# Five products of the first expert's first layer in another order, in a fused state-space scan and expert layer

## The chip, the cores and the metric

The kernel runs on one core of one Trainium2 chip. The metric is the device time of one execution, in microseconds (us); less is better. In the views below PE is TensorE's matmul, PEld its weight load, DVE is VectorE, ACT is ScalarE, POOL is GpSimd, and SP is SyncE, which only issues DMAs here.

## What is computed

First comes a chunked state-space scan (its result y has 3072 rows of 256 numbers), then an expert layer: every token goes to one of eight experts by a hash of its number, and through that expert's two matrices.

```python
# scan, 4 x 8 heads, 768 steps in chunks of 32
L = np.exp(cum[:, :, :, None] - cum[:, :, None, :]) * causal
y_intra = np.einsum('bhij,bhjd->bhid', CB * L, xc)
y_inter = np.einsum('bhin,bhnd->bhid', Cc, state) * decay_to_i[..., None]
...
# experts: x is (3072, 256), w1[e] is 256 x 1024, w2[e] is 1024 x 256
expert_idx = token_ids * np.int64(2654435761) % np.int64(E)
for e in range(E):
    xe = x[expert_idx == e]
    out[expert_idx == e] = np.maximum(xe @ w1[e], 0.0) @ w2[e]
```

All matmuls of the expert layer are in float32.

## The kernel before

Up to about 74 us the core computes the scan, works out which token goes where, and writes y to DRAM. POOL's indirect DMAs (`gather`, line 628) bring the rows of y back in the order of the experts, 128 rows to a tile; PE transposes them (`turn_x`, line 636) and ACT copies them into `xT`, which holds the tokens as columns. The experts are sorted by their number of tokens into places p = 0 to 7. Place p has two halves of `HALF[p]` columns: 202 for place 0, 200 for place 1.

Each matrix product of an expert is a product of 2 x 2 blocks: two halves of the inputs, two halves of the outputs, two halves of the tokens. It is computed with seven block products in place of eight. They work on sums of weight blocks (`sums_w`, line 782: `s[0]` to `s[3]`) and on differences of token blocks (`sums_x`, line 882), which build on each other:

```python
# sums_x: a, b of t[i] = a - b; q(k, j) is input half k of token half j
a_, b_ = ((q(0, 1), q(0, 0)), (q(1, 1), t[:, 0]), (q(0, 1), q(1, 1)), (q(1, 0), t[:, 1]))[i]
```

In `up` (line 903), the first layer, product 1 and 2 use tokens as they are, 5 uses `s[0]` and `t[0]`, 6 uses `s[1]` and `t[1]`, 7 uses `s[2]` and `t[2]`, 4 uses a weight block and `t[3]`, 3 uses `s[3]` and tokens. Each product is made in two halves (`q0` = 0 and 2), of two matmuls each; a float32 matmul shows as two records in the profile. I call them 5a and 5b and so on. The a halves use PSUM banks 0 and 1, the b halves 2 and 3: products 1, 2, 5 and 3 stand in bank 0 (2), products 6, 7 and 4 in bank 1 (3), where 7 adds onto 6 and 4 onto 7. Each result is read before the next product adds onto it: after 6 (`u2`, line 932) and 7 (`u3`, line 935) DVE adds product 1's part, then product 5's bank and `u3` give a block of the hidden layer (line 944), 4 gives another (line 941), 3 the third (line 939). ACT applies the relu to the first two (lines 945, 942).

For the first four places, products 1 and 2 are made early, while DVE still makes weight sums (line 1049; bank `i % 6`). The last four of these halves belong to place 3: its a half stands in bank 0, its b half in bank 1, and ACT reads them (product 2: line 927).

Then `step(p)` (line 1059) walks over the places. It puts the first layer of place p beside the second layer of place p - 1 (`down`, line 964) on PE, in an order written out in lists: `UP_E` (line 1056) has the five products that are left for the first four places. Step 0 has no second layer beside it: its rounds are a half a, a transposed tile of place 1's tokens, a half b (lines 1081 and 1091). Between them `step` puts the differences for the next place (`sums_x(1, i)`, line 1107) on DVE, and weight sums for later on POOL. In step 1, `sums_h` (lines 891 to 898) makes the differences of the hidden layer of place 0 on DVE. The order on each engine is the order in which this code is written; waits between engines are set by the tiles and banks that instructions share.

Of the kernel before, what the change touches and what calls it, by code (L numbers as in the profile page):

```python
# [20 lines left out]
NEAR = 4  # L21
# [4 lines left out]
def kernel(  # L26
# [20 lines left out]
    E, _, F = moe_w1.shape  # L47
# [564 lines left out]
    def load_w1(p, i, eng=sp_e):  # L612
        if p not in w1s:
            w1s[p] = (w4[0] if p % 4 == 3 else wpool).tile([P, DP, F], F32, name="w1")
        src = moe_w1[bass.ds(regs[p], 1), :, i * FH:(i + 1) * FH].rearrange("e (k p) f -> p (e k) f", p=P)
        eng.dma_start(out=w1s[p][:, :, i * FH:(i + 1) * FH], in_=src)

    def load_w2(p, eng=sp_e):
        w2s[p] = wx[0].tile([P, FP, DM], F32, name="w2", bufs=2)
        eng.dma_start(out=w2s[p], in_=moe_w2[bass.ds(regs[p], 1)].rearrange("e (k p) d -> p (e k) d", p=P))  # L620
# [144 lines left out]
    def sums_w(p, layer, i, eng):  # L765

        if layer == 1:
            w = w1s[p]
            q = lambda i, k: w[:, k, i * FH:(i + 1) * FH]
            if p not in s1:  # L770
                s1[p] = (spool if p % 3 else s1pool).tile([P, 4, FH], F32, name="s1")
            s = s1[p]
        else:
            w = w2s[p]
            q = lambda i, k: w[:, k * Q4:(k + 1) * Q4, i * P:(i + 1) * P]
            if p not in s2:
                s2[p] = spool.tile([P, 4, Q4, P], F32, name="s2")
            s = s2[p]
        i = (2, 1, 3, 0)[i]
        a_, b_, o = ((q(1, 0), q(1, 1), OP.add), (s[:, 2], q(1, 1), OP.add), (q(1, 0), q(0, 0), OP.subtract),  # L780
                     (q(0, 1), s[:, 1], OP.subtract))[i]
        eng.tensor_tensor(out=s[:, i], in0=a_, in1=b_, op=o)  # L782
        if eng is pool_e and i in (0, 3):
            eng.tensor_copy(out=space, in_=s[:, i, 0, 0:1] if layer == 2 else s[:, i, 0:1])
# [90 lines left out]
    def sums_x(p, i):  # L875
        n = HALF[p]
        q = lambda k, j: xT[:, k, slots(p, j)]
        if i == 0:
            t1[p] = mwork.tile([P, 4, N0], F32, name="t1")
        t = t1[p][:, :, 0:n]  # L880
        a_, b_ = ((q(0, 1), q(0, 0)), (q(1, 1), t[:, 0]), (q(0, 1), q(1, 1)), (q(1, 0), t[:, 1]))[i]
        dve.tensor_tensor(out=t[:, i], in0=a_, in1=b_, op=OP.subtract)  # L882

    def sums_h(p, i):
        n = HALF[p]
        if i == 0:
            t2[p] = hpool.tile([P, 4, Q4, N0], F32, name="t2", bufs=1)
        t = t2[p][:, :, :, 0:n]
        q = lambda k, j: hx[p][:, {(0, 1): 0, (1, 0): 1, (1, 1): 2}[k, j], :, 0:n]
        if i == 0:  # L890
            dve.scalar_tensor_tensor(out=t[:, 0], in0=q(0, 1), scalar=0.0, in1=h11[p][:, :, 0:n],
                                     op0=OP.max, op1=OP.subtract)
        elif i == 1:
            dve.tensor_tensor(out=t[:, 1], in0=q(1, 1), in1=t[:, 0], op=OP.subtract)
        elif i == 2:
            dve.scalar_tensor_tensor(out=t[:, 2], in0=q(0, 1), scalar=0.0, in1=q(1, 1), op0=OP.max, op1=OP.subtract)  # L896
        else:
            dve.tensor_tensor(out=t[:, 3], in0=q(1, 0), in1=t[:, 1], op=OP.subtract)
# [90 lines left out]
    def put(k, bank=OB, at=0, eng=None):  # L989
        for i in range(DP):  # L990
            pe.transpose(out=ps[:, bank, at + i * P:at + (i + 1) * P], in_=xT[:, i, k * P:(k + 1) * P], identity=ident)  # L991
        o_sb = mwork.tile([P, DM], F32, name="o_sb", bufs=10)
        if eng is dve:
            dve.tensor_copy(out=o_sb, in_=ps[:, bank, at:at + DM])
        else:
            act.activation(o_sb, ps[:, bank, at:at + DM], AF.Copy)  # L996
        return o_sb, idx_out[:, k:k + 1]

    def scatter(o_sb, idx):
        st = pool_e.indirect_dma_start(  # L1000
            out=out[:], out_offset=bass.IndirectOffsetOnAxis(ap=idx, axis=0),
            in_=o_sb, in_offset=None, bounds_check=NT - 1, oob_is_err=False)
        tc.declare_no_dep(st.ins, group="out_rows", reason="distinct rows")
        tc.add_to_no_dep_group("out_rows", st.ins)
# [6 lines left out]
    def ask(ks):  # L1011
        for k in ks:
            if k not in asked:
                gather(k)
                asked.add(k)

    def turn(k):
        if k not in turned:
            turn_x(k, XB)
            turned.add(k)  # L1020
# [33 lines left out]

    UP = [1, 6, 2, 7, 5, 4, 3]
    UP_E = [6, 7, 5, 4, 3]
    DOWN = [1, 2, 6, 5, 7, 4, 3]

    def step(p):

        ups = [] if p == E else UP_E if p < NEAR else UP
        downs = DOWN if p > 0 else []
        turns = [k for k in need(p + 1) if k not in turned]
        puts = [k for k in outs if done_at[k] == p - 2]
        gets = [k for w in ((2,), (3, 4))[p] for k in need(w) if k not in asked] if p < 2 else need(p + 3)
        sums = [(p, 2, i) for i in range(4)] if p < E else []
        sums += [(p + 2, 1, i) for i in range(4)] if 0 < p < E - 2 else []
        xs_ = [(p + 1, i) for i in range(4)] if p + 1 < E else []
        R = 5 if p == 0 else 7
        off = 0 if p == 0 else (R - len(ups)) // 2  # L1070
        sent = []
        for r in range(R):
            if p > 0 and (r == 0 or p >= NEAR and r < 4):
                sums_h(p - 1, r)
            if sent:
                scatter(*sent.pop(0))
            if gets and p == 0:
                ask(gets)
                gets = []
            if 0 <= r - off < len(ups):  # L1080
                up(p, 0, ups[r - off])
            if turns:
                turn(turns.pop(0))
            if puts:
                sent.append(put(puts.pop(0)))
            if sums and not (p == 1 and r < 4):
                sums_w(*sums.pop(0), pool_e)
            if gets and r >= 1:
                ask([gets.pop(0)])
            if 0 <= r - off < len(ups):  # L1090
                up(p, 2, ups[r - off])
            if 0 < p < NEAR and 0 < r < 4:
                sums_h(p - 1, r)
            if sums and r == 3 and p != 1:
                sums_w(*sums.pop(0), pool_e)
            if p >= NEAR and r >= 3 and not turns and xs_:
                sums_x(*xs_.pop(0))
            if p == 1 and r == 4:
                pool_e.tensor_copy(out=space, in_=t2[0][:, 3, 0, 0:1])
            if p == E - 1 and r == R - 1:  # L1100
                sums_h(p, 0)
            if downs:
                down(p - 1, downs[r])
                if downs[r] == 4 and p + 1 < E:
                    load_w2(p + 1)
            if p < NEAR and r >= (2 if p == 0 else 3) and not turns and xs_:
                sums_x(*xs_.pop(0))
        while xs_ or turns:
            if turns:
                turn(turns.pop(0))  # L1110
            else:
                sums_x(*xs_.pop(0))
        for o in sent:
            scatter(*o)
        for v in sums:
            sums_w(*v, pool_e)
        if p + 4 < E:
            load_w1(p + 4, 0)
            load_w1(p + 4, 1)
        for k in gets:  # L1120
            ask([k])

    for p in range(E):
        step(p)
# [136 lines left out]
```

## Time and profile before

| what | us |
|---|---|
| median of 3 runs | 235.72 |
| the runs | 231.1, 235.72, 237.67 |
| the profiled execution | 231.41 |
| its span, first to last instruction | 229.7 |
| PE busy | 213.5 (93%) |
| DVE busy | 180.7 (79%) |
| POOL busy | 172.4 (75%) |
| ACT busy | 89.4 (39%) |

The mean granted clock of TensorE is 0.992 of full speed in this execution. Times in the rows below count from the start of the span. A row of the timeline gives a start, a length, the engine, the line, the operation with the tiles that it writes and reads, how many instructions in a row it stands for, and in brackets the idle time ahead of it with what ended that. Lengths of PE's rows overlap, since matmuls are pipelined: the pace is read from one start to the next.

### The profile page before, as it was taken

The numbers are of one execution on the slowest core, as the hardware profiler recorded it, in microseconds if no ns is written. First come the engines' busy times: TensorE is split into PE (matmuls) and PEld (weight loads), VectorE is DVE, ScalarE is ACT, GpSimd is POOL, SyncE is SP. The second block draws the span as 40 slices with busy tenths as digits, with TensorE's granted clock in tenths as the row PEclk, the third lists the DMA queues.
The fourth block names the chain that finished last, engine by engine and source line by source line (L and its number), as shares of the span: only waits on it lengthen the run. The fifth ranks groups of instructions, "written<-read, shape, count | busy, mean of one in ns | idle before, by whom it ended". The sixth has DMA issues, their size and how long they took to land.

```text
span 229.7 us, 5853 instructions
## 1 busy us (share of the span) xinstructions
PE 213.5 (93%) x2266; PEld 200.5 (87%) x2266; DVE 180.7 (79%) x314; ACT 89.4 (39%) x190; POOL 172.4 (75%) x220
## 2 busy tenths in 40 slices
PE   6889989998786899999999999999999999999990
PEld 2778878877685799999999999999999999999980
DVE  7868899798547688899997998697489979956630
ACT  4774965954443551312123214234323411413210
POOL 7977367866717198489988998999799999996342
PEclk9999999999999999999999999999999999999996
DMA  6999799999888885029019119307005112401011
GB/s 136 162 200 127 181 191 177 174 185 302 273 218 259 253 267 199 24 75 332 30 62 334 64 47 339 118 7 244 26 24 204 33 45 79 175 23 47 24 70 43
DMA packets 49877, 33.16 MB, mean 144 GB/s; under 512 B 26632, under 2 KB 44184, under 8 KB 49850
## 3 DMA queue, kind: packets, MB, share of 16 engines
q1 hardware_dynamic: 46786, 25.76, 45.6%
q0 software_dynamic: 2400, 6.43, 8.5%
q10 hardware_dynamic: 664, 0.61, 1.1%
q8 instruction: 18, 0.29, 0.5%
q14 instruction: 9, 0.07, 0.1%
HBM read 26.49 MB, written 6.42 MB: 143 GB/s over the span
## 4 chain that ended last, share of the span: by engine, by line
PE 73%; DMA 8%; DVE 7%; ACT 6%; issue 2%; SPq 1%; POOL 1%; ACTq 0%; DVEq 0%; POOLq 0%
PE ps L964 31%; PE ps L917 28%; PE ps L315 4%; DMA w<-in_moe_w_dram 3%; DMA xg<-y_tokens,idx_in 3%; PE ps L991 2%; PE ps L374 2%; PE ps L636 2%; DMA y_tokens<-y_sb 2%; DVE m L321 1%; ACT z L358 1%; PE ps L387 1%; PE ps L269 1%; DVE rows L259 1%; ACT ct L289 1%
## 5 line engine op out<-in xcount | busy, mean ns | idle before, releaser
L628 POOL DMA_INDIRECT xg<-y_tokens,idx_in x25 | 30.2, 1206 | 17.1 <-issue 10.1
L917 PE MATMUL ps<-t,s 128*128 128x202 f32 (+7 forms) x192 | 37.1, 328 | 0.6 <-DVE t L882 0.6
L782 POOL TENSOR_TENSOR s<-w 128x512 f32<-128x512 f32 x26 | 33.2, 1277 | 5.7 <-DMA w<-in_moe_w_dram 5.5
L1000 POOL DMA_INDIRECT out_dram<-o_sb,idx_out x25 | 26.4, 1056 | 12.5 <-ACT o_sb L996 6.7
L964 PE MATMUL ps<-t,s 128*128 128x202 f32 (+7 forms) x192 | 35.5, 326 | 0.0
L917 PEld LDWEIGHTS ps<-t,s 128*128 128x128 f32 x192 | 31.5, 190 | 1.3 <-ACT h L927 0.9
L964 PEld LDWEIGHTS ps<-t,s 128*128 128x128 f32 x192 | 31.8, 189 | 0.3 <-issue 0.3
L917 PE MATMUL ps<-xT,w 128*128 128x200 f32 (+7 forms) x128 | 24.9, 329 | 3.0 <-DMA w<-in_moe_w_dram 2.3
L917 PEld LDWEIGHTS ps<-xT,w 128*128 128x128 f32 x128 | 20.7, 190 | 3.8 <-DVE s L782 2.5
L945 ACT ACTIVATE hx<-hx 128x404 f32<-128x404 f32 (+7 forms) x16 | 8.3, 525 | 31.8 <-DVE hx L944 31.3
L321 DVE COPY_PREDICATED m<-cmask,ps 128x1024 f32<-128x1024 int32 x12 | 15.5, 1320 | 3.6 <-PE ps L315 3.6
L782 POOL TENSOR_TENSOR s<-w,s 128x512 f32<-128x512 f32 x13 | 17.6, 1351 | 0.5
L782 POOL TENSOR_TENSOR s<-s,w 128x512 f32<-128x512 f32 x13 | 17.3, 1327 | 0.5
L882 DVE TENSOR_TENSOR t<-xT 128x202 f32<-128x202 f32 (+7 forms) x16 | 16.4, 1024 | 0.8 <-ACT xT L642 0.8
L923 ACT ACTIVATE p<-ps 128x404 f32<-128x404 f32 (+7 forms) x16 | 7.9, 492 | 20.0 <-PE ps L917 19.7
L374 PEld LDWEIGHTS ps<-x_t,m 128*64 128x64 f32 x384 | 12.1, 138 | 3.0 <-issue 1.3
L374 PE MATMUL ps<-x_t,m 128*64 128x64 f32 x384 | 13.4, 224 | 1.1 <-ACT y_sb L401 0.6
L315 PE MATMUL ps<-ce,bt 32*64 32x128 f32 x384 | 12.9, 274 | 1.1 <-ACT ce L289 0.7
L882 DVE TENSOR_TENSOR t<-xT,t 128x202 f32<-128x202 f32 (+7 forms) x16 | 13.7, 854 | 0.0
L896 DVE SCALAR_TENSOR_TENSOR t<-hx 128x808 f32<-128x808 f32 (+7 forms) x8 | 13.3, 1660 | 0.0
L315 PEld LDWEIGHTS ps<-ce,bt 32*64 32x64 f32 x384 | 10.4, 132 | 2.5 <-ACT ce L289 0.9
L358 ACT ACTIVATE z<-z,half 128x256 f32<-128x256 f32 x22 | 10.0, 504 | 6.6 <-DVE z L352 6.6
(201 smaller groups left out, 472.5 us busy)
## 6 DMA issues: line engine op xcount, KB each, us to landing
w<-in_moe_w_dram SPq DMA_DIRECT2D x16, 512.0 KB, 7.1
w<-in_moe_w_dram SPq DMA_DIRECT2D x8, 1024.0 KB, 8.0
x_t<-in_x_dram SPq DMA_DIRECT2D x12, 256.0 KB, 6.2
y_tokens<-y_sb SPq DMA_DIRECT2D x10, 256.0 KB, 4.3
raw<-in_B_dram SPq DMA_DIRECT2D x12, 128.0 KB, 3.5
raw<-in_C_dram SPq DMA_DIRECT2D x12, 128.0 KB, 3.5
y_tokens<-y_sb ACTq DMA_DIRECT2D x2, 256.0 KB
xg<-y_tokens,idx_in POOLq DMA_INDIRECT x25, 3.5
```

Source lines behind the costliest of these rows:

```text
L315: pe.matmul(out=ps[u * T:(u + 1) * T, GB + g, b * P:(b + 1) * P].rearrange("q (e i) -> q e i", e=2), lhsT=bts[ck][r, b, c], rhs=ces[ck][r, ...
L321: dve.copy_predicated(out=m_sb[k % 2][:, g0:g1].rearrange("q g b i -> q g (b i)"), mask=cmask.bitcast(I32).rearrange("q j i -> q (j i)").u ...
L358: act.activation(z4s[un][:, :, j], zs[un].rearrange("q b e d -> q b (e d)"), AF.Copy, scale=half4[:, j:j + 1])
L374: pe.matmul(out=o, lhsT=m_sb[k % 2][:, g, b, e * T:(e + 1) * T], rhs=xs[k][:, b, 2 * g + e], start=first(g // 2 * 2 + b % 2, c), stop=True ...
L628: pool_e.indirect_dma_start(out=xg[k], out_offset=None, in_=y_dram[0:n, :], in_offset=bass.IndirectOffsetOnAxis(ap=idx_in[:, k:k + 1], axi ...
L782: eng.tensor_tensor(out=s[:, i], in0=a_, in1=b_, op=o)
L882: dve.tensor_tensor(out=t[:, i], in0=a_, in1=b_, op=OP.subtract)
L896: dve.scalar_tensor_tensor(out=t[:, 2], in0=q(0, 1), scalar=0.0, in1=q(1, 1), op0=OP.max, op1=OP.subtract)
L917: pe.matmul(out=ps[:, bank, i * n:(i + 1) * n], lhsT=lhs[:, (q0 + i) * P:(q0 + i + 1) * P], rhs=rhs, start=(first and i == 0), stop=True, ...
L945: act.activation(hq(2), hq(2), AF.Relu)
L964: pe.matmul(out=ps[:, bank, 0:n], lhsT=lhs(q), rhs=rhs(q), start=(first and q == 0), stop=True, skip_group_check=True)
L1000: st = pool_e.indirect_dma_start(out=out[:], out_offset=bass.IndirectOffsetOnAxis(ap=idx, axis=0), in_=o_sb, in_offset=None, bounds_check= ...
```

## The change

Step 0 takes its five products from a list of its own, 5, 6, 7, 4, 3 in place of 6, 7, 5, 4, 3. Places 1 to 3 keep the order that they had.

```diff
     UP = [1, 6, 2, 7, 5, 4, 3]
     UP_E = [6, 7, 5, 4, 3]
+    UP_0 = [5, 6, 7, 4, 3]
     DOWN = [1, 2, 6, 5, 7, 4, 3]
 
     def step(p):
 
-        ups = [] if p == E else UP_E if p < NEAR else UP
+        ups = [] if p == E else UP_0 if p == 0 else UP_E if p < NEAR else UP
```

On PE, the rows of step 0 read alike but for their waits. Here they are of before, from the first product of step 0 on (`t_1435` are the token differences of place 0, `s_1274` its weight sums, `w_1037` its weights; line 636 transposes):

```order
L917 MATMUL ps<-t_1435,s_1274 128x202 [waits DVE_49,Activation_49]
L917 MATMUL ps<-t_1435,s_1274 128x202
L636 MATMUL ps<-ident,xg 128x128 [waits DMASW1_49]
L636 MATMUL ps<-ident,xg 128x128
L917 MATMUL ps<-t_1435,s_1274 128x202 x2
L917 MATMUL ps<-t_1435,s_1274 128x202 [waits DVE_49]
L917 MATMUL ps<-t_1435,s_1274 128x202
L636 MATMUL ps<-ident,xg 128x128 [waits DMASW2_49,Activation_49]
L636 MATMUL ps<-ident,xg 128x128
L917 MATMUL ps<-t_1435,s_1274 128x202 [waits DVE_49]
L917 MATMUL ps<-t_1435,s_1274 128x202 x5
L917 MATMUL ps<-t_1435,w_1037 128x202 [waits DMAHW2_49,DVE_49]
```

These are 6a, transposes, 6b, 7a, transposes, 7b with 5a and 5b behind it, and 4a. Now, in the same place:

```order
L917 MATMUL ps<-t_1435,s_1274 128x202 x2
L917 MATMUL ps<-t_1435,s_1274 128x202 [waits DVE_49,Activation_49]
L917 MATMUL ps<-t_1435,s_1274 128x202
L636 MATMUL ps<-ident,xg 128x128 [waits DMASW2_49,Activation_49]
L636 MATMUL ps<-ident,xg 128x128
L917 MATMUL ps<-t_1435,s_1274 128x202 x2
L917 MATMUL ps<-t_1435,s_1274 128x202 [waits DVE_49]
L917 MATMUL ps<-t_1435,s_1274 128x202
L917 MATMUL ps<-t_1435,s_1274 128x202 [waits DVE_49]
L917 MATMUL ps<-t_1435,s_1274 128x202
L917 MATMUL ps<-t_1435,w_1037 128x202 [waits DMAHW2_49,DVE_49]
```

The piece begins with 5b; ahead of it stand 5a and its transposes. 6a, which waits for DVE and ACT, is now the third half; 7a, 7b and 4a follow each other, each with a wait for DVE, where 7b had 5a and 5b between it and 4a.

On DVE, the sums behind these products (`u` are the results of products 6 and 7 with product 1 added, `hx` the hidden layer, `t_1483` the token differences of place 1):

```order
-L932 TENSOR_TENSOR u_1450<-ps,p_1343 128x404
-L932 TENSOR_TENSOR u_1459<-ps,p_1353 128x404
-L935 TENSOR_TENSOR u_1463<-ps,p_1343 128x404
-L935 TENSOR_TENSOR u_1471<-ps,p_1353 128x404
-L944 TENSOR_TENSOR hx<-ps,u_1463 128x404
+L932 TENSOR_TENSOR u_1459<-ps,p_1343 128x404
+L932 TENSOR_TENSOR u_1467<-ps,p_1353 128x404
+L935 TENSOR_TENSOR u_1471<-ps,p_1343 128x404
 L944 TENSOR_TENSOR hx<-ps,u_1471 128x404
+L935 TENSOR_TENSOR u_1479<-ps,p_1353 128x404
+L944 TENSOR_TENSOR hx<-ps,u_1479 128x404
 L882 TENSOR_TENSOR t_1483<-xT 128x200
```

The sum of product 5 with `u3` (line 944) comes between the readings of 7a and 7b (line 935), where it came after both. ACT, POOL and SP have the same instructions in the same order as before.

## Rows read from the trace of the kernel before

**Rows 1.** The page's first part: busy us, share of the span, instructions.
```profile
PE 213.5 (93%) x2266; PEld 200.5 (87%) x2266; DVE 180.7 (79%) x314; ACT 89.4 (39%) x190; POOL 172.4 (75%) x220
```

**Rows 2.** Waits of PE, 78 to 230 us: who for whom, us, times, longest.
```profile
PE ps L917 <- DVE t L882: 0.6, 1, 0.6
PE ps L1137 <- DVE xT L1167: 0.4, 1, 0.4
```

**Rows 3.** One window: length; busy (count) of PE, PEld, DVE, ACT, POOL; clock; DMA.
```profile
77.89:85.50 7.61, 7.61 (x46) 7.37 (x47) 5.53 (x11) 2.93 (x6) 4.57 (x5) 1.00 0.91 303
```

**Rows 4.** The chain of waits around 77 us: start, us, what.
```profile
76.93 0.94 DVE t L882 x3
```

**Rows 5.** Timeline of DVE, 72 to 104 us.
```profile
76.53 0.37 DVE L882 TENSOR_TENSOR t<-xT 128x202 f32<-128x202 f32 x1 [0.82 <-ACT xT L642]
76.93 0.37 DVE L882 TENSOR_TENSOR t<-xT,t 128x202 f32<-128x202 f32 x1
...
78.95 0.58 DVE L932 TENSOR_TENSOR u<-ps,p 128x404 f32<-128x404 f32 x1 [1.09 <-PE ps L917]
79.78 0.58 DVE L932 TENSOR_TENSOR u<-ps,p 128x404 f32<-128x404 f32 x1 [0.26 <-PE ps L917]
...
82.16 1.26 DVE L944 TENSOR_TENSOR hx<-ps,u 128x404 f32<-128x404 f32 x2
83.33 0.36 DVE L882 TENSOR_TENSOR t<-xT 128x200 f32<-128x200 f32 x1
...
86.77 0.99 DVE L891 SCALAR_TENSOR_TENSOR t<-hx,h 128x808 f32<-128x808 f32 x1
...
89.01 1.00 DVE L894 TENSOR_TENSOR t<-hx,t 128x808 f32<-128x808 f32 x1
```

**Rows 6.** Timeline of PE and, last, PEld, 72 to 104 us.
```profile
77.89 0.95 PE L917 MATMUL ps<-t,s 128*128 128x202 f32 x4 [0.58 <-DVE t L882]
78.68 0.38 PE L636 MATMUL ps<-ident,xg 128*128 128x128 f32 x2
78.89 1.64 PE L917 MATMUL ps<-t,s 128*128 128x202 f32 x8
...
80.58 2.22 PE L917 MATMUL ps<-t,s 128*128 128x202 f32 x12
...
85.37 0.38 PE L636 MATMUL ps<-ident,xg 128*128 128x128 f32 x2
...
91.04 1.53 PE L964 MATMUL ps<-t,s 128*128 128x202 f32 x8
...
77.89 0.64 PEld L917 LDWEIGHTS ps<-t,s 128*128 128x128 f32 x4 [0.88 <-ACT h L927]
```

**Rows 7.** Timeline of ACT, 72 to 104 us.
```profile
76.69 0.49 ACT L927 ACTIVATE h<-ps 128x384 f32<-128x384 f32 x1 [0.27 <-PE ps L917]
77.34 0.49 ACT L927 ACTIVATE h<-ps 128x384 f32<-128x384 f32 x1 [0.16 <-PE ps L917]
```

**Rows 8.** DMA issues, 72.4 to 73 us: count, us from issue to landing.
```profile
xg<-y_tokens,idx_in POOLq DMA_INDIRECT x1, 2.8
```

**Rows 9.** Timeline of POOL, 72 to 104 us.
```profile
83.42 1.41 POOL L782 TENSOR_TENSOR s<-w,s 128x512 f32<-128x512 f32 x1
...
85.07 1.27 POOL L782 TENSOR_TENSOR s<-w 128x512 f32<-128x512 f32 x1
...
87.18 1.50 POOL L628 DMA_INDIRECT xg<-y_tokens,idx_in  x1 [0.56 <-PE ps L964]
```

**Rows 10.** Timelines of DVE and POOL at two later places.
```profile
118.58 1.99 DVE L882 TENSOR_TENSOR t<-xT 128x192 f32<-128x192 f32 x1
...
119.05 1.29 POOL L782 TENSOR_TENSOR s<-w 128x512 f32<-128x512 f32 x1
...
104.39 2.07 DVE L891 SCALAR_TENSOR_TENSOR t<-hx,h 128x800 f32<-128x800 f32 x1
...
104.32 1.28 POOL L782 TENSOR_TENSOR s<-s,w 128x512 f32<-128x512 f32 x1
```

## The prediction

> **What bounds the kernel now.** The first view is the page with its busy times: TensorE (PE) is busy 213.5 of 229.7 us [rows 1]. The second is the list of waits from 78 us to the end: in all of it PE is kept waiting twice, 0.6 us before a product of line 917 and 0.4 us in the tail [rows 2]. From the first expert's products to the tail the kernel is therefore one unbroken row of products; the window of those first products shows PE busy for all of its 7.61 us at the full clock, 1.00, which is 2.4 GHz [rows 3]. What PE gains at the beginning of this row moves the end, as long as nothing that PE waits for comes late. The change works on the first of the two waits, so 0.6 us is about the most that it has to win.
>
> Who ends this wait is told in two ways. The chain of waits leads through three token differences of line 882, from 76.93 to 77.87, and then to the product at 77.89 [rows 4]. But product 6 reads only the second difference, t[1], which starts at 76.93 and takes 0.37, so that it is done at 77.30 [rows 5]. The weight load of the same product, on PEld, names ACT h of line 927 [rows 6]. That is the right one: product 6 opens bank 1, and bank 1 still holds the last early product, which ScalarE (ACT) reads from 77.34 for 0.49 us, to 77.83 [rows 7]. The product starts 0.06 later. t[1] alone would have let it start at about 77.35.
>
> **The change, part by part.** Nothing is added or removed. Ten half products, each of two matmuls in the order and four records in the profile, change places on PE; on VectorE (DVE) the sums behind them change with them; ACT, GpSimd (POOL) and SP keep their order. I follow PE and DVE step by step with these durations. A half product takes 0.69 (seven between 80.58 and 85.37, in 4.79), and 0.10 more when it had to wait (0.79 between 77.89 and 78.68); two transposes take 0.21 (78.68 to 78.89) [rows 6]. DVE reads a half product 0.89 after that product's start (78.89 to 79.78) and takes 0.58 for it [rows 5, 6]. A reader on another engine starts 0.05 to 0.06 after the end it waits for.
>
> 1. The wait at 77.89. Product 5 needs t[0], done at 76.53 + 0.37 = 76.90 [rows 5], and bank 0, which ACT has read at 76.69 + 0.49 = 77.18 [rows 7]. It starts at 77.24: minus 0.65. The chance of this step is high, but what gives it is the bank, more than the difference of tokens. The transposes behind the first half move up to 78.03; their gathers were issued before 72.57, and the one of that time landed after 2.8, at 75.4 [rows 8], so they are there. Half 5b, in bank 2, starts at 78.24, 6a at 78.93 (its bank 1 is free since 77.83), the other transposes at 79.62, 6b at 79.83.
>
> 2. Products 7 and 4. 7a adds onto 6a in bank 1, so DVE must have read 6a: 79.88 + 0.58 = 80.46, and 7a starts at 80.52 without a stall. 7b needs the reading of 6b, 80.72 + 0.58 = 81.30: it would be ready at about 81.21 and starts at 81.35, with the 0.10 of a restart: plus 0.24. 4a adds onto 7a in the same bank and needs it read. Before, four half products lay between 7a and 4a, and 5a and 5b with 4a still between 7b and 4b; now one does. 7a is read at 81.50 + 0.58 = 82.08, 4a starts at 82.14, again with a restart: plus 0.10. Then DVE has the final sum of product 5 in its order (from 82.11), before the reading of 7b (82.61 to 83.19): 4b, ready at 82.93, starts at 83.24: plus 0.31 and 0.10. 3a follows at 84.03, 3b at 84.72, and the two transposes that stood at 85.37 [rows 6] stand at 85.40. The sum of 1 and 2: -0.65 + 0.24 + 0.10 + 0.41, and with roundings +0.03. The wait is not removed; it is cut in three and put where DVE's reading comes between two products of one bank. The bounds: -0.65, if DVE's reads hide as they do before; +0.40, if each of the four readings stalled PE by 0.16 more, one restart and one hand-over.
>
> 3. The second expert's token differences. DVE's row is now later: its last sum of products 5 and 7 ends at 83.80 where it ended at 83.42 before (82.16 + 1.26) [rows 5]. Behind it in DVE's order stands t[0] of the second expert. Before, it took 0.36 at 83.33, just ahead of a weight sum that POOL began at 83.42 [rows 5, 9]. Now it comes at about 83.7, inside that sum. The nearest rows: a difference that began 0.47 before POOL's sum at 119.05 took 1.99 and ended 0.23 after that sum [rows 10]; those of 76.53 and 83.33 took 0.37 and 0.36 [rows 5]. So the price of meeting a weight sum lies between 0 and 1.63, and I take it by the first row, as the POOL instruction is already running: t[0] ends 0.23 after POOL's sum (83.42 + 1.27), at 84.92. t[1] meets the next sum (85.07, 1.27) [rows 9] in the same way and ends at about 86.44. Then come the sums of product 3 (to 87.53), the last two differences, and line 891 at 88.0, where it was 86.77 [rows 5]. Of this lag of 1.2 most is slack: PE's product 6 of the second expert waits only for t[1] and starts at 86.98. What is late next is line 894, which was at 89.01 [rows 5]: now 90.15 to 91.15, and the first expert's product 6 of the second layer, which stood at 91.04 [rows 6], waits for it to 91.20, with a restart: plus 0.25. The rest of the lag I expect DVE to make up in its idle time behind that, where it waits for products as at 78.95 and 79.78. Bounds of this term: 0 and the 1.35 of the second rival.
>
> The Trainium skill, SBUF — State Buffer, section "Who interferes with whom", has a rule for this: a VectorE instruction with two SBUF inputs and a GpSimd instruction that reads SBUF exclude each other, and whichever issues first keeps the port for its whole length. The row at 118.58 agrees with it; that at 83.33 shows no price, as it came first. By the rule the hold is the full rest of POOL's sum, and the sum comes out as above, +0.28; by the row at 83.33 alone it would be +0.03.
>
> **The sum.** +0.03 + 0.25 = +0.28 us. The profiled execution took 231.41 us around a span of 229.7, so 231.7 for one like it. The runs shown are 231.1, 235.72 and 237.67: they differ by 6.6 us, twenty times the sum, and nothing in this change touches what sets them apart as far as the profile shows. On their median I get 236.0.
>
> **Rivals.**
> A. The gain stays: PE starts 0.65 earlier and DVE's readings hide, as the same order of engines lets them in the row before, where PE waits for nothing after 78 us [rows 2]. For it: DVE is busy only 5.53 of 7.61 us in this window [rows 3]. Against it: DVE needs 0.58 for each reading and PE 0.69 for each half, and products of one bank now follow each other directly. 231.41 - 0.65 = 230.8; on the median 235.1.
> B. Slower: DVE is held once more, at line 891 of the first expert, place 88 us. With a POOL weight sum beside it that line took 2.07 at 104.39 instead of 0.99 [rows 5, 10]. It decides as soon as line 891 begins after a weight sum and not beside a gather. The price: line 894 ends 1.08 later, PE waits for it at 91.04 to 92.28, with a restart 1.35 in place of 0.25: 232.8; on the median 237.1. Against it: at 88 us POOL is in its gathers, and the line 891 of 86.77 took its 0.99 beside the gather of 87.18 [rows 5, 9].
> C. The change does not do what it says: if the first product's bank were the only thing waited for and bank 0 came no earlier, PE would start at 77.89 as before, and steps 2 and 3 would add 0.65 + 0.28: 232.3. Against it: ACT reads the banks in order, 0.65 apart [rows 7].
>
> **How the numbers follow.** Forecast 0.6, A 0.22, B 0.1, C 0.03, something else 0.05. All the cases lie within 1% of each other, so the sign is open but the size is not; about 2% is what a measurement of this kernel can tell from no change. The time: 236.0, on the median. The range is that of the runs, with the cases' ends: 231.1 - 0.65, about 230.4, to 237.67 + 0.28, about 238.0. Faster by over 2%: 0.05, slower by over 2%: 0.04, both only because runs differ by up to 2.8%; within 2%: 0.91.
>
> **What would show it.** Right: the wait at 77.89 gone, the first product 5 at about 77.24 behind ACT's first h of line 927; PE waits before line 917 at about 81.3, 82.1 and 83.2, ended by DVE's lines 932 and 935; the transposes of the second step within 0.1 of 85.4; t[0] of the second expert over 1 us long. Wrong: transposes at 84.8 or earlier (A); line 891 over 1.5 us and PE waiting at 91 for over 1 us (B); a first product at 77.89 (C). A difference of several us that comes from before 76 us would have nothing to do with my steps.

## The result and the profile after

The changed kernel takes 235.73 us (median of 14 runs, 232.68 to 238.87), the kernel before, measured beside it, 235.10 (median of 14, 231.1 to 238.12): ratio 1.010, interval 1.0052 to 1.0148. That is +0.63 us by the medians, within the 2% that count as no change. The ratio takes only runs near the fastest of each kernel, and of the kernel before that fastest run, 231.1, lies 1.3 us below its next. A second comparison (the run e6 below), in which both kernels took longer, gave 239.26 (13 runs) against 239.68 (23 runs), ratio 1.0023, interval 0.9983 to 1.0063.

The profiled execution has a span of 230.8 us where it was 229.7. The busy times on its page, to be held against [rows 1]:

```profile
PE 214.8 (93%) x2266; PEld 200.6 (87%) x2266; DVE 181.3 (79%) x314; ACT 89.2 (39%) x190; POOL 171.6 (74%) x220
```

The list of waits of PE from 78 us to the end (who for whom, us, times, longest) answers to [rows 2]: the wait of 0.6 at line 917 is gone, and one of 0.4 at line 964, the second layer, has come.

```profile
PE ps L1138 <- DVE xT L1168: 0.4, 1, 0.4
PE ps L964 <- DVE t L894: 0.4, 1, 0.4
```

PE's timeline answers to [rows 6] (start, us, engine, line, operation, count; in brackets idle time before and what ended it):

```profile
76.38 1.47 PE L917 MATMUL ps<-xT,w 128*128 128x192 f32 x8
77.78 0.95 PE L917 MATMUL ps<-t,s 128*128 128x202 f32 x4
...
82.68 2.05 PE L917 MATMUL ps<-t,w 128*128 128x202 f32 x8
...
85.93 0.38 PE L636 MATMUL ps<-ident,xg 128*128 128x128 f32 x2
...
92.15 1.61 PE L964 MATMUL ps<-t,s 128*128 128x202 f32 x8 [0.39 <-DVE t L894]
```

The first of these rows are the last eight records of the early products, which the change doesn't touch. In the kernel before they stand here:

```profile
75.84 1.47 PE L917 MATMUL ps<-xT,w 128*128 128x192 f32 x8
```

So 0.54 of the 1.1 us between the two spans was there before the first changed instruction: PE's wait ahead of this row, which both traces put down to a landing of weights, is as long as before (2.25 and 2.27 us) and ended that much later (74.36 against 73.82). I call the start of this row S, and all times in the table below count from S, by which executions can be laid side by side. S itself lay anywhere from 75.84 to 87.67 in the thirteen profiles.

PEld's timeline shows where the new waits stand, which PE's rows hide in their groups; its first row has the old wait, 0.23 in place of 0.88 [rows 6]:

```profile
77.78 0.64 PEld L917 LDWEIGHTS ps<-t,s 128*128 128x128 f32 x4 [0.23 <-ACT h L927]
...
81.89 0.64 PEld L917 LDWEIGHTS ps<-t,s 128*128 128x128 f32 x4 [0.19 <-DVE u L932]
...
82.68 0.64 PEld L917 LDWEIGHTS ps<-t,w 128*128 128x128 f32 x4
...
83.78 0.64 PEld L917 LDWEIGHTS ps<-t,w 128*128 128x128 f32 x4 [0.46 <-DVE u L935]
```

The others are 7b (81.89), 4a (82.68, whose small wait has no bracket) and 4b (83.78). Each starts 0.05 after DVE's reading of the product that stood in its bank (the next view, DVE's timeline: 81.26 + 0.58 = 81.84, then 7b; 82.05 + 0.58 = 82.63, then 4a; 83.16 + 0.57 = 83.73, then 4b; line 944 stands between the last two readings).

```profile
81.26 0.58 DVE L932 TENSOR_TENSOR u<-ps,p 128x404 f32<-128x404 f32 x1 [0.26 <-PE ps L917]
82.05 0.58 DVE L935 TENSOR_TENSOR u<-ps,p 128x404 f32<-128x404 f32 x1 [0.21 <-PE ps L917]
82.66 0.58 DVE L944 TENSOR_TENSOR hx<-ps,u 128x404 f32<-128x404 f32 x1
83.16 0.57 DVE L935 TENSOR_TENSOR u<-ps,p 128x404 f32<-128x404 f32 x1
...
84.25 0.75 DVE L882 TENSOR_TENSOR t<-xT 128x200 f32<-128x200 f32 x1
...
85.90 0.61 DVE L882 TENSOR_TENSOR t<-xT,t 128x200 f32<-128x200 f32 x1
...
87.97 0.98 DVE L891 SCALAR_TENSOR_TENSOR t<-hx,h 128x808 f32<-128x808 f32 x1
...
89.84 2.16 DVE L894 TENSOR_TENSOR t<-hx,t 128x808 f32<-128x808 f32 x1
```

The last four rows are DVE beside POOL's weight sums, which answer to [rows 9]: t[0] and t[1] take 0.75 and 0.61 in place of 0.36, line 891 its usual 0.98, and line 894 takes 2.16 where it took 1.00 [rows 5].

```profile
83.51 1.27 POOL L782 TENSOR_TENSOR s<-w,s 128x512 f32<-128x512 f32 x1
...
85.02 1.27 POOL L782 TENSOR_TENSOR s<-w 128x512 f32<-128x512 f32 x1
...
89.85 1.28 POOL L782 TENSOR_TENSOR s<-w 128x512 f32<-128x512 f32 x1
```

### The profile page after: what moved, and what is told of

It reads as the page before. It is cut to its first block, busy times and chain, and to the rows that moved or that the text cites. A ratio compares the mean times of both kernels' runs of the same rounds, so it can differ in the third digit from the quotient of the medians.

```text
span 230.8 us, 5852 instructions
## 1 busy us (share of the span) xinstructions
PE 214.8 (93%) x2266; PEld 200.6 (87%) x2266; DVE 181.3 (79%) x314; ACT 89.2 (39%) x190; POOL 171.6 (74%) x220
## 4 chain that ended last, share of the span: by engine, by line
PE 70%; DVE 12%; DMA 7%; ACT 5%; issue 2%; SPq 1%; POOL 0%; DVEq 0%; POOLq 0%; ACTq 0%
PE ps L964 30%; PE ps L917 26%; PE ps L315 4%; DMA w<-in_moe_w_dram 3%; DVE m L321 3%; DMA xg<-y_tokens,idx_in 3%; PE ps L991 2%; PE ps L374 2%; PE ps L636 2%; ACT z L358 1%; PE ps L387 1%; PE ps L269 1%; DVE t L894 1%; DVE rows L259 1%; DMA a_in<-in_a_dram 1%
## 5 line engine op out<-in xcount | busy, mean ns | idle before, releaser
L628 POOL DMA_INDIRECT xg<-y_tokens,idx_in x25 | 29.5, 1181 | 17.4 <-issue 7.3
L932 DVE TENSOR_TENSOR u<-ps,p 128x404 f32<-128x404 f32 (+7 forms) x16 | 8.7, 554 | 5.6 <-PE ps L917 5.2
```

Of the source, the lines that this page charges most:

```text
L628: pool_e.indirect_dma_start(out=xg[k], out_offset=None, in_=y_dram[0:n, :], in_offset=bass.IndirectOffsetOnAxis(ap=idx_in[:, k:k + 1], axi ...
L932: dve.tensor_tensor(out=st["u2"], in0=src, in1=st["p1"], op=OP.add)
```

## The experiments

Times from S, in us: the start of the first product, of the transposes of the second step, and of the first expert's product 6 of the second layer (line 964, "down 6"); where DVE was held beside a weight sum (an instruction that took over 0.2 more than it does alone); and the end of the span.

| execution | first | transposes | down 6 | DVE held at | end |
|---|---|---|---|---|---|
| before | 2.05 | 9.53 | 15.20 | - | 153.88 |
| before, e8 | 2.05 | 9.53 | 15.86 | t[0], t[1], line 894 | 154.62 |
| changed | 1.40 | 9.55 | 15.77 | t[0], t[1], line 894 | 154.41 |
| changed, e6 | 1.40 | 9.55 | 15.98 | t[0], t[1], line 894 | 154.64 |
| e1 | 1.61 | 9.06 | 14.73 | - | 153.43 |
| e2 | 2.05 | 10.26 | 16.36 | t[3] | 155.01 |
| e3 | 1.40 | 9.29 | 16.07 | t[0], t[3] | 154.72 |
| e4 | 1.40 | 9.55 | 15.22 | - | 153.42 |
| e9 | 1.40 | 8.88 | 14.61 | line 894 | 153.26 |
| e10 | 1.40 | 8.88 | 16.23 | t[0], t[3] | 154.88 |

From down 6 to the end it is 138.64 to 138.76 in every row but that of e4 (138.20; it leaves out work of POOL). So what moves down 6 moves the end by as much.

**e1: the old order, with the a half's two banks exchanged.** From the kernel before:

```diff
-                up(p, 0, ups[r - off])
+                up(p, 0, ups[r - off], banks=(1, 0) if p == 0 else None)
```

> The order of before (6, 7, 5, 4, 3), but in step 0 the a halves use banks 0 and 1 the other way round: 6, 7 and 4 in bank 0, 5 and 3 in bank 1. All times from S, the start of the last row of eight early product records (75.84 in before, 76.38 in the changed kernel). Bank theory (ScalarE's reading of bank 1 ended the wait): the first product starts 1.51 after S, when the second difference is done, where before had 2.05; the first transposes of step 1 stand at 9.0 (before 9.53), without new waits of PE; the kernel is about 0.5 us faster than before. Difference theory (VectorE's differences ended the wait): the first product stays at 2.05 and nothing changes.

PE's timeline, then DVE's for t[1]:

```profile
80.56 1.47 PE L917 MATMUL ps<-xT,w 128*128 128x192 f32 x8
82.17 0.92 PE L917 MATMUL ps<-t,s 128*128 128x202 f32 x4
...
89.62 0.38 PE L636 MATMUL ps<-ident,xg 128*128 128x128 f32 x2
```

```profile
81.65 0.37 DVE L882 TENSOR_TENSOR t<-xT,t 128x202 f32<-128x202 f32 x1
```

Product 6 still comes first, but in the bank that ACT frees first, and starts at 1.61 in place of 2.05: the wait for t[1] that is left is 0.21 above the earliest start (1.40). It came 0.10 later than expected, because t[1] ends at 82.02 and the product that reads it starts 0.15 later (82.17), not 0.05 as behind a bank that has been read. The row behind it is before's own and keeps the gain: 9.06. As a whole e1 took 235.64 (12 runs) against 235.65 (17), ratio 1.0005, interval 0.995 to 1.006.

**e2: the new order, with the same exchange.** The same edit in the changed kernel.

> The changed order (5, 6, 7, 4, 3) with the two banks of the a halves exchanged in step 0, so that product 5 comes first and opens bank 1. Bank theory: the first product waits for ScalarE's second reading and starts 2.05 after S, as in before, though the first difference is done at 1.06; the transposes of step 1 stand at 10.1 to 10.2 (9.55 in the changed kernel). Difference theory: the first product starts 1.40 after S as in the changed kernel.

DVE, ACT and PE, each from its own timeline:

```profile
80.27 0.37 DVE L882 TENSOR_TENSOR t<-xT 128x202 f32<-128x202 f32 x1 [0.38 <-ACT xT L642]
```

```profile
81.09 0.49 ACT L927 ACTIVATE h<-ps 128x384 f32<-128x384 f32 x1 [0.16 <-PE ps L917]
```

```profile
79.58 1.47 PE L917 MATMUL ps<-xT,w 128*128 128x192 f32 x8
81.63 0.95 PE L917 MATMUL ps<-t,s 128*128 128x202 f32 x4 [0.58 <-ACT h L927]
...
89.84 0.38 PE L636 MATMUL ps<-ident,xg 128*128 128x128 f32 x2
```

Its t[0] is done at 80.64, and yet product 5 starts at 81.63, 0.05 after ACT's second reading (81.58): at 2.05, as before. The new order in the late bank gains nothing and pays for the waits behind it: transposes at 10.26. Its one time is 236.35.

**e3: the changed kernel, with both sums of line 944 behind the readings of product 7.**

```diff
+        if p == 0 and what == 7:
+            if q0 == 0:
+                return
+            for r0 in (0, 2):
+                o, s_ = hx[p][:, 2, r0:r0 + 2, 0:n], sts[p, r0]
+                dve.tensor_tensor(out=o, in0=s_["z"], in1=s_["u3"], op=OP.add)
+                act.activation(o, o, AF.Relu)
+            return
```

> The changed kernel with VectorE's final sum of product 5 (a half) put behind its reading of 7b in step 0. Theory: 4b no longer waits for that sum; it starts 7.15 after S (7.40 in the changed kernel) and the transposes of step 1 come at 9.2 to 9.3 (9.55). But the first expert's product 6 of the second layer still waits for VectorE's line 894, which is no earlier, and starts 15.7 to 15.8 after S as in the changed kernel (15.77): the kernel gains nothing. Rival: the loss is PE's waits in step 0 alone; then that product comes 0.3 earlier too, at 15.5, and so does the end.

4b starts at 7.13 in place of 7.40, the transposes at 9.29 in place of 9.55, so the 0.27 that line 944 cost PE are shown. But down 6 came at 16.07, later than either side expected. The hold of DVE had moved to t[3] of the second expert, and PE waited for what stands behind it (DVE's timeline, then PE's):

```profile
88.89 2.09 DVE L882 TENSOR_TENSOR t<-xT,t 128x200 f32<-128x200 f32 x1
```

```profile
92.48 1.62 PE L917 MATMUL ps<-t,s 128*128 128x200 f32 x8 [0.83 <-DVE u L932]
```

**e4: the changed kernel, POOL's second-layer weight sums of places 0 and 1 replaced by constants.**

```diff
+        if eng is pool_e and layer == 2 and p < 2:
+            eng.memset(s[:, i], 0.01)
+            return
```

> The changed kernel with POOL's weight sums of the second layer of places 0 and 1 replaced by memsets of the same tiles, which read no SBUF (the second layer of these two experts is then computed with constants in place of the weight sums). Hold theory: the token difference after VectorE's last sum of product 5 takes 0.36 instead of 0.75 and line 894 takes 1.0 instead of 2.16; product 6 of the second layer starts 15.2 to 15.3 after S (15.77 in the changed kernel) and PE no longer waits for line 894. Rival (the lag comes from VectorE's own order): line 894 still ends too late and PE waits as before, 15.6 or more.

DVE's timeline for t[0] of the second expert and, later, line 897; then the waits of PE from 78 us:

```profile
88.05 0.36 DVE L885 TENSOR_TENSOR t<-xT 128x200 f32<-128x200 f32 x1
...
93.36 0.99 DVE L897 TENSOR_TENSOR t<-hx,t 128x808 f32<-128x808 f32 x1
```

```profile
PE ps L1141 <- DVE xT L1171: 0.4, 1, 0.4
```

(Its lines stand 3 further down: 885 and 897 are 882 and 894.) All differences take 0.35 to 0.36, line 894 takes 0.99, the wait at line 964 is gone, and down 6 is back at 15.22, against 15.20 before. So the whole lateness of down 6 in the changed kernel comes from DVE beside POOL's work, and without that the new order costs 0.02. The edit takes away more than the sums: memsets need not wait for weights, and POOL has no instruction here from 82.51 to 99.94, no gather either. That the sums are what holds DVE is read from where held instructions end, each at a set distance behind a sum (see the part on the prediction).

**e5, e9, e10: only the first half product moved.** From the kernel before; 5a comes first and 5b stays between 7b and 4a:

```diff
+    UP_0 = [(0, 5), (0, 6), (2, 6), (0, 7), (2, 7), (2, 5), (0, 4), (2, 4), (0, 3), (2, 3)]
...
-                up(p, 0, ups[r - off])
+                up(p, *(UP_0[2 * r] if p == 0 else (0, ups[r - off])))
...
-                up(p, 2, ups[r - off])
+                up(p, *(UP_0[2 * r + 1] if p == 0 else (2, ups[r - off])))
```

> Step 0 in the order 5a, 6a, 6b, 7a, 7b, 5b, 4a, 4b, 3a, 3b: 5a opens bank 0 early, as in the change, but 5b stays between 7b and 4a, as in before. All times from S. Theory: the first product starts at 1.40 without the changed kernel's waits at 7b, 4a and 4b; the transposes of step 1 come at 8.8 to 8.9 (9.53 in before, 9.55 in the changed kernel, 9.06 with exchanged banks), and product 6 of the second layer at 14.5 to 14.6 if VectorE is not held by POOL, up to 0.6 later if it is. Measured as a whole about 0.5 us faster than before, which is less than runs differ. Rival: VectorE's readings bound step 0 in any order that starts early; then the transposes stay at 9.3 or later.

In e5's profile the clock was at 0.50 from 83.3 to 90.1, over S and up to the first product (90.05), so it does not show when that product starts; as a whole e5 took 240.56 (12 runs) against 239.68 (23), ratio 1.0021, interval 0.9969 to 1.0073. Two more profiles follow.

> The order 5a, 6a, 6b, 7a, 7b, 5b, 4a, 4b, 3a, 3b again, as the profile of its first run had TensorE at 1.2 GHz from 83.3 to 90.1 us, over its first product. Theory: at full clock the first product starts 1.40 after S and the transposes of step 1 come at 8.8 to 8.9 (7.4 after the first product, as in the first run: 7.43); product 6 of the second layer at 14.5, or up to 0.7 later where POOL holds VectorE. Rival: transposes at 9.3 or later.

> The same kernel once more, so that one of the two profiles has the full clock in step 0: 1.40, 8.8 to 8.9, and 14.5 to 15.2 after S.

PE's timeline in e9:

```profile
82.92 1.47 PE L917 MATMUL ps<-xT,w 128*128 128x192 f32 x8
84.31 0.95 PE L917 MATMUL ps<-t,s 128*128 128x202 f32 x4
...
91.80 0.38 PE L636 MATMUL ps<-ident,xg 128*128 128x128 f32 x2
...
97.53 1.61 PE L964 MATMUL ps<-t,s 128*128 128x202 f32 x8
```

The transposes come at 8.88, 0.65 ahead of before: the full first gain, and nothing given back. In e9 it reaches the end (153.26 against 153.88). e10 has the same row of products up to the transposes, and ends 1.62 later. Its DVE and POOL timelines show why:

```profile
98.83 2.09 DVE L882 TENSOR_TENSOR t<-xT,t 128x200 f32<-128x200 f32 x1
```

```profile
98.37 1.01 POOL L628 DMA_INDIRECT xg<-y_tokens,idx_in  x1 [0.30 <-PE ps L964]
99.41 1.28 POOL L782 TENSOR_TENSOR s<-w 128x512 f32<-128x512 f32 x1
```

**e6, e7, e8: both kernels again.**

> The changed kernel once more. Theory: from S, the products of step 0 and the transposes of step 1 (9.55) repeat within 0.05, as only TensorE, ScalarE and VectorE's readings set them; which SBUF difference POOL holds, and with it product 6 of the second layer (15.2 to 16.1), changes with the time at which POOL's weight sums begin after S (4.43 in the first profile). As a whole 0 to 1 us slower than before. Rival: the first measurement (ratio 1.010) holds for a cause that the profile pair does not show; then the ratio is 1.005 or more again.

> The kernel before once more, for the same question: from S, the first product at 2.05 and the transposes of step 1 at 9.53 again; if POOL's weight sums begin at another time after S than 4.87, one of VectorE's differences may be held here too, and product 6 of the second layer comes between 15.2 and 16.0. If before keeps 15.20 at another phase of POOL, its VectorE has slack that the changed kernel lacks.

> The kernel before a third time, as a second sample for the same question: 2.05, 9.53, and product 6 of the second layer between 15.2 and 16.0 after S.

e7 fell under the lower clock (0.50 from 82.6 to 86.0), so it has no place in the table. But its first product, at 86.75, comes after that, and from there on it can be read. PE's and DVE's timelines:

```profile
86.75 0.95 PE L917 MATMUL ps<-t,s 128*128 128x202 f32 x4 [0.58 <-ACT h L927]
...
100.90 1.61 PE L964 MATMUL ps<-t,s 128*128 128x202 f32 x8
```

```profile
95.83 2.09 DVE L882 TENSOR_TENSOR t<-xT,t 128x200 f32<-128x200 f32 x1
```

Here the kernel before is held at t[3], and down 6 comes 14.15 after the first product, where it was 13.15 in the first profile of before (77.89 to 91.04 [rows 6]). For the same old wait this trace names ACT's h, not DVE's t. e8 is the telling one: the kernel before, with its old row of products, its wait of 0.58, and the hold at line 894. PE's, DVE's and POOL's timelines:

```profile
84.14 1.47 PE L917 MATMUL ps<-xT,w 128*128 128x192 f32 x8
...
86.19 0.95 PE L917 MATMUL ps<-t,s 128*128 128x202 f32 x4 [0.58 <-DVE t L882]
...
100.01 1.61 PE L964 MATMUL ps<-t,s 128*128 128x202 f32 x8 [0.50 <-DVE t L894]
```

```profile
91.64 1.23 DVE L882 TENSOR_TENSOR t<-xT 128x200 f32<-128x200 f32 x1
...
97.69 2.17 DVE L894 TENSOR_TENSOR t<-hx,t 128x808 f32<-128x808 f32 x1
```

```profile
91.37 1.28 POOL L782 TENSOR_TENSOR s<-w,s 128x512 f32<-128x512 f32 x1
...
97.72 1.28 POOL L782 TENSOR_TENSOR s<-w 128x512 f32<-128x512 f32 x1
```

In the first profile of before, t[0] began at 7.49 and the weight sum at 7.58: it slipped in 0.09 ahead [rows 5, 9]. In e8 t[0] came at 7.50 and the sum at 7.23. POOL's sums stood 0.35 earlier, and before paid what the changed kernel pays: down 6 at 15.86, end 154.62, against 154.41 and 154.64.

**e11: e1 again.**

> The order of before with exchanged banks again, at another phase of POOL: first product 1.61 and transposes 9.06 after S, as in its first profile; product 6 of the second layer between 14.7 (no hold) and 15.4 (held as in the third profile of before, where it came 0.66 later).

Its clock was 0.51 from 79.3 to 86.2, over S and up to just before the first product (86.56), so it says nothing of e1's gain.

## Why the prediction was right or wrong

**The time.** Forecast 236.0 and no change; measured 235.73 and no change. That the median lay so near is in part luck: the forecast stood on a median of three runs, 235.72, where fourteen gave 235.10, and it added 0.28 where the medians differ by 0.63. The first made the forecast too high, the second too low.

**Step 1 was right, and for the reason given.** Product 5 starts at 1.40 from S, as worked out (77.24 for an S of 75.84), 0.65 earlier. That the bank and not the difference of tokens ended the old wait is shown from two sides: e1 takes away 0.44 of the wait without changing the order, and e2 keeps all of it with the new order. The name in the list of waits, DVE t of line 882, was the wrong one for before; PEld's ACT h was right. One figure was off: a product starts 0.15 after the difference that it reads (e1), not 0.05, so that t[1] alone would have let the old first product start at about 77.45, not 77.35.

**Step 2 was right in its times.** From S the forecast had 7b at 5.51, 4a at 6.30, 4b at 7.40 and the transposes at 9.56; the trace has 5.51, 6.30, 7.40 and 9.55. The gain is given back in three waits for DVE's readings. The written sum is not right, though: -0.65 + 0.24 + 0.10 + 0.41 is +0.10, and it is not rounding that makes it +0.03. Before takes 1.48 for the two half products from 78.89 to 80.37 [rows 6]; the changed kernel takes 1.38 for its two there (78.78 to 80.16). So the new order saves 0.10 there: the step's times have that gain, but it is no term of its sum. Measured from S, the transposes come 0.02 later. Two lesser figures don't come out either, and nothing rests on them: four stalls of 0.16 are 0.64, not 0.40, and t[1] would by the step's own rule end at 86.57 (85.07 + 1.27 + 0.23), not 86.44. e9 and e10 show the other side: with 5b between 7b and 4a nothing is given back. Rival A, in which the gain stays, is refuted for this order and holds for theirs, up to the transposes.

**Step 3 is where the prediction failed,** in size and in whose cost it is. The direction holds: t[0] comes 0.38 later, falls inside POOL's sum and is held, t[1] too, and down 6 waits for line 894. But t[0] took 0.75, not over 1 us, which the prediction had named as a sign of being right: POOL's sum began 0.45 earlier from S (7.13 against 7.58), and less of it was left. The term that was too small is the 0.25 for line 894. The step let that line begin at 90.15 and take 1.00, merely late, and did not ask what POOL does there. In the trace of before POOL's next sum runs over that place:

```profile
90.02 1.28 POOL L782 TENSOR_TENSOR s<-w 128x512 f32<-128x512 f32 x1
```

In the changed kernel line 894 began only 0.29 later from S than before (13.46 against 13.17), met this sum (line 894 from 89.84, the sum from 89.85), took 2.16, and down 6 came 0.57 later than in the first profile of before. Rival B had foreseen one more hold on a long instruction and its length (1.08; it was 1.16), but at line 891, which took 0.98, and its 1.35 for PE was too much.

Two readings behind the step were off. First, I took from [rows 10] that a held instruction ends 0.23 after the sum. That is so for differences, 0.36 long (85.02 + 1.27 = 86.29; t[1] ends at 86.51). Line 894, 1.00 long, ended 0.87 after it (91.13 and 92.00), and so did line 891 in [rows 10] (105.60 and 106.46). What these share is that the instruction ends its own length, less 0.12 to 0.14, after the sum, as if it did nearly all its work behind it. The Trainium skill, SBUF — State Buffer, section "Who interferes with whom", says that a VectorE instruction with two SBUF inputs contends with a GpSimd instruction that reads SBUF, that the lock is exclusive, and that the order of issue decides who blocks. The 2.16 at line 894 agrees with the exclusive lock. The order can't be read from the starts in the trace alone: line 894 began 0.01 ahead of the sum and was held, and the row at 118.58, which the prediction counted for the rule, began 0.47 ahead of its sum and was held. Where t[0] began 0.06 to 0.13 ahead (before, e1 and e9), it took its 0.35 to 0.36, and the sum took 1.36 to 1.43 in place of 1.27.

Second, I charged the hold to the change. In the executions here that are held at line 894 or not at all, down 6 starts about 0.15 after the end of line 894 or at its place in PE's own row, whichever is later: line 894 ends at 15.62 in the changed kernel (down 6 at 15.77), 15.72 in e8 (15.86), 15.83 in e6 (15.98); in the first profile of before it ends at 14.17, and PE's row decides (15.20). So DVE has 0.88 to spare, and a hold of a long instruction takes more than that. Whether it comes goes with where POOL's sums fall: the first of them began 4.87 after S in the first profile of before, and at 4.43, 4.63 and 4.52 in the changed kernel, e6 and e8. In before, the changed kernel and e8 the trace names a landing of weights as what this first sum waited for (in e6 a copy on ACT). The changed DVE row is 0.38 later at this place; that it therefore slips in ahead less easily is argued, not shown. Before is held as well, in e8 and e7, and at no smaller cost: 0.66 (15.86 against 15.20) and 1.00, where the changed kernel is 0.55 and 0.76 behind e4. Between equals the change is worth +0.02 (e4 against before) or -0.09 and +0.12 (15.77 and 15.98 against e8's 15.86).

**What stays open.** The first comparison's 1.010 is more than the pair of traces explains: 0.53 us from S on is 0.23%, and the medians of that comparison differ by 0.27%. It did not come again (1.0023). S alone moved by 11.8 us between profiles, all of it ahead of the change, and no run here shows what moves it. How often each kernel is held is not known either: two full profiles of each, with e7, are too few. e1 and the half-product order reach down 6 0.5 to 0.6 sooner when DVE is not held for long, but no total shows it (1.0005, 1.0021).

## What to carry to other kernels

Before a product is moved to be ready sooner, see which of its conditions ended the wait: end times and the weight load's row say it where one wait carries two semaphores. Products that add onto one bank wait for the reading between them: here one more half product in the gap (e9, e10) hid the reading, and bringing them together gave back what the earlier start had won. Where VectorE and GpSimd both work from SBUF, a change of some tenths of a us can be swallowed or doubled by when GpSimd's instructions fall: compare from a common mark, in several profiles of both kernels, before a hold is charged to the change.

## What was not expected of the hardware

A hold can come through a gather. In e10 the difference at 98.83 began while POOL was in a gather (98.37 to 99.38) and was held to 100.92, 0.23 after the weight sum that follows directly (99.41 + 1.28). The row at 118.58 in [rows 10] is of the same kind, and t[3] is held in the same way in e2, e3, e5, e7 and e11, each time 0.46 to 0.52 after the start of a gather with a sum directly behind it. It is not every instruction that begins in such a gather: line 894 of before began at 89.01, 0.03 after a gather's start, with the sum of 90.02 directly behind, and took its 1.00 [rows 5]. What decides between the two is not shown. Two differences of e9, inside a gather with another gather behind it (92.79 and 93.07), took 0.35 and 0.36.

TensorE's clock fell to 0.50, that is 1.2 GHz, near the changed place in e5, e7 and e11. The windows of e5 (length; busy and count of PE, PEld, DVE, ACT, POOL; clock; DMA share; GB/s):

```profile
73.00:80.00 7.00, 6.94 (x43) 6.82 (x44) 2.12 (x5) 4.04 (x8) 2.66 (x3) 1.00 0.90 244
80.00:83.30 3.30, 0.77 (x5) 0.47 (x4) 3.23 (x6) 1.00 (x2) 2.69 (x3) 1.00 0.72 266
83.30:90.10 6.80, 6.16 (x21) 6.01 (x22) 3.44 (x8) 2.12 (x5) 0.09 (x1) 0.50 0.70 221
90.10:100.00 9.90, 9.90 (x61) 9.71 (x60) 7.44 (x14) 4.10 (x9) 8.30 (x9) 1.00 0.63 205
```

PE was busy for 0.77 of 3.30 us while it waited for the early weight sums, and the lower level came shortly before it was at work again (83.94); it rose after 6.8 us in which PE was busy for 6.16. In e8 a wait of 2.7 at the same place brought no fall (from 79 to 88 us its clock stood at 1.00).
